# A decode attention block on one core: the tile steps as hardware loops of three tiles, and the rest as straight code ordered by a small tracker

## Chip, cores, metric

The kernel runs on one core of a Trainium2 chip. The metric is the device time of one execution in microseconds.

## The reference, cut to what matters

One token for each of two batch rows goes through cached attention with 32 heads, through a small mixer with an MLP, and the two results are mixed by a gate.

```python
B, Sq, D = 2, 1, 1024;  H, Sk, Dh = 32, 16384, 128
q = x @ wq
scores = einsum("bhqd,bhkd->bhqk", q, k_cache) * Dh ** -0.5
o = einsum("bhqk,bhkd->bhqd", softmax(scores), v_cache)
a = o @ wo
x1 = x + shifted(gelu(layernorm(x) @ w1)) @ w2        # one position: the shifted rows are all zero
b = x1 + gelu(layernorm(x1) @ w3) @ w4
out = g * a + (1 - g) * b                             # g = sigmoid(sum(x * gate_w))
```

The two caches are 537 MB in bf16, the weights some 36 MB. All of it is read once.

## The kernel before

The work is cut into 32 tiles of one batch row and two heads. A tile is one load of K and one of V, 8.39 MB each, and the loads go through three SBUF slots. VectorE transposes K in 16 pieces; PE multiplies each piece into the score bank S; then come the maximum, the exponentials and a transpose of the probabilities. While K of tile i+1 is scored, V of tile i is weighed.

```python
    def qk_stage(i):
        Kw = kn_tiles.pop(i)[:].bitcast(FP32)
        z = z_tiles[i % NZ]
        S = sps.tile([P, NC_], FP32, name="S")            # two score banks
        for m in range(NM):                               # NM = 16
            T = t_tile([P, 2, CJ, 32], FP32)              # two T buffers, in turn
            moved = nc.vector.transpose(out=T[:]..., in_=Kw[:, m * CW : (m + 1) * CW]...)
            for v in range(4):
                nc.tensor.matmul(S[:], lhsT=z[:, v, NM - 1 - m : NM - 1 - m + P], rhs=Tb[:, v // 2, :, v % 2],
                                 start=(m == 0 and v == 0), stop=(m == NM - 1 and v == 3))
    ...
    for i in range(-1, NT):                               # NT = 32, written out by Python: straight code
        if i + 1 < NT:
            xfers.append(("big", f"k{i + 1}", lambda i=i: load_k(i + 1)))
            steps.append((f"k{i + 1}", lambda i=i: (build_z(i + 1), qk_stage(i + 1))))
        if i >= 0:
            xfers.append(("big", f"v{i}", lambda i=i: load_v(i)))
            steps.append((f"v{i}", lambda i=i: pv_stage(i)))
        if i + 1 < NT:
            steps.append(("", lambda i=i: softmax_stage(i + 1)))
        if i in extra:                                    # w1 and w2 after tile 4, w3 after tile 8
            ...
```

The load of w2 is deliberately uneven: 216 of its 1024 rows go by a DMA whose slowest dimension is 3.

```python
    WAYS, QUAD, BASE, MORE = 3, 4, 6, 18
        nc.sync.dma_start(out=w2[:, 0:BASE, :], in_=B_w2[0 : P * BASE, :]...)
        nc.sync.dma_start(out=w2[W2_MORE, BASE : BASE + MORE, :],
            in_=B_w2[r0 : r0 + n_more, :].rearrange("(y x r) n -> x y (r n)", x=WAYS, y=QUAD))
        nc.sync.dma_start(out=w2[W2_REST, BASE, :], in_=B_w2[r0:D, :])
```

## Time and profile before

| | before |
|---|---|
| device time, median | 1334.2 us |
| span in the profile | 1332.4 us |
| DMA engines busy with data | 99.4% |
| PE / VectorE busy | 60% / 57% |
| last weight piece landed, first and last engine | 1321.4 and 1328.8 us |

The page's head, its 40 slices and its DMA queues. In the queue lines the columns are packets, MB, and the time of the packets as a share of the span of 16 engines.

```profile
span 1332.4 us, 11498 instructions
PE 797.2 (60%) x4982; PEld 354.1 (27%) x5045; DVE 760.4 (57%) x1005; ACT 27.2 (2%) x68; POOL 12.8 (1%) x40
...
DMA  9999999999999999999999999999999999999998
...
q1 hardware_dynamic: 11165, 572.53, 99.4%
q8 instruction: 39, 0.64, 0.2%
q14 instruction: 11, 0.09, 0.0%
```

Read the DMA line first: no slice of the span has the engines idle. PE (PEld is the loading of its weights) and VectorE (DVE) are each busy for under two thirds of it. The second thing to see is q8: instructions too are fetched by these DMA engines, 39 packets of 16 KB. They are taken here as those of PE's straight code of 10,162 instructions (5,045 weight loads, as many matmuls, 72 others), because the counts fit: between the packets at 84.9 and 1298.8 us PE starts 9,205 instructions, and 36 packets come, 255.7 instructions to each. So a packet is 256 instructions of 64 bytes; the sizes of loop bodies are estimates from that.

One tile on VectorE, from the timeline (start, duration, what, and in brackets the idle time before it and what ended that):

```profile
633.59 2.37 DVE L384 STREAM_TRANSPOSE T<-Kn 128x1024 f32<-128x1024 f32 x2 [6.85 <-DMA Kn<-in_A_k_cache_dram]
636.89 1.25 DVE L384 STREAM_TRANSPOSE T<-Kn 128x1024 f32<-128x1024 f32 x1 [0.93 <-PE S L398]
638.40 15.65 DVE L384 STREAM_TRANSPOSE T<-Kn 128x1024 f32<-128x1024 f32 x13 [0.27 <-PE S L398]
655.21 0.69 DVE L409 TENSOR_REDUCE m<-S 128x1 f32<-128x512 f32 x1 [1.15 <-PE S L398]
658.83 0.35 DVE L453 TENSOR_SCALAR Os<-O,xmask 128x128 f32<-128x128 f32 x1 [2.94 <-PE O L442]
...
665.01 0.17 DVE L477 RECIPROCAL rinv<-misc 128x2 f32<-128x2 f32 x1 [0.74 <-PE misc L251]
672.24 2.37 DVE L384 STREAM_TRANSPOSE T<-Kn 128x1024 f32<-128x1024 f32 x2 [7.06 <-DMA Kn<-in_A_k_cache_dram]
```

VectorE idles 7.06 us until the next K has landed. The period is 38.65 us, which is two loads of 19.3 us.

The view of waits (engine and line, what was waited for, us in total, times, longest):

```profile
DVE T L384 <- DMA Kn<-in_A_k_cache_dram: 203.8, 30, 12.5
```

A third reading comes from the times of the DMAs' semaphore updates in the trace. Each load of K or V, and each of the last weight pieces, posts 16 updates, read here as one for each engine that has finished its share. Sorted, for the last weight piece of the kernel before, in us of the span:

```
1321.42 1321.47 1321.75 1321.99 | 1326.91 1327.32 1327.46 1327.56 1328.08 1328.21 1328.35 1328.38 1328.40 1328.48 1328.65 1328.80
```

Four engines are done 5 to 7 us before the others. A load is complete only with its last engine (the first update for the K of the tile above comes at 628.05 us, the sixteenth at 633.57, and VectorE starts at 633.59), so the end of the kernel follows the most loaded engine and not the mean. How the engines came apart can be followed. After the first instruction packet, at 31.7 us, one engine finishes the next load 1.82 us behind the first and 1.25 behind the last but one; the weights before it came within 0.6. From there the spread is 2 us until the uneven w2 load, 5.5 us right after it (three engines late), and then the other nine catch up with those three over the remaining millisecond and mostly pass them, to 7.4 us.

### The profile page before, as it was taken

How to read it: one execution, taken by the hardware profiler on the slowest of the kernel's cores; microseconds unless marked ns; L12 is line 12 of the kernel's file. 1: busy time of each engine (PE TensorE's matmuls, PEld its weight loads, DVE VectorE, ACT ScalarE, POOL GpSimd, SP SyncE). 2: the span in 40 equal slices, each digit the busy share in tenths (PEclk: the TensorE clock that was granted, in tenths of full speed). 3: DMA queues.
4: the chain of work that ended last, by engine and by line, in shares of the span. 5: the costliest groups of instructions: out<-in, count | busy, mean ns of one | idle time of the engine just before them, and what ended most of it. 6: DMA issues, size and time to landing. Idle time of an engine off the chain costs nothing.

```text
span 1332.4 us, 11498 instructions
## 1 busy us (share of the span) xinstructions
PE 797.2 (60%) x4982; PEld 354.1 (27%) x5045; DVE 760.4 (57%) x1005; ACT 27.2 (2%) x68; POOL 12.8 (1%) x40
## 2 busy tenths in 40 slices
PE   2576655766556755556665555566655556655554
PEld 1223222322225322222222222222222222222222
DVE  1677665466653665555666555566655556665540
ACT  0000000000000000000000000000000000000000
POOL 0000000000000000000000000000000000000000
PEclk9788877787777777788887777888777788877776
DMA  9999999999999999999999999999999999999998
GB/s 410 439 437 435 422 437 432 426 435 433 437 428 441 431 422 439 439 437 425 431 436 433 439 429 437 424 439 433 433 431 438 438 424 435 437 437 430 431 427 340
DMA packets 11221, 573.27 MB, mean 430 GB/s; under 512 B 1252, under 2 KB 1260, under 8 KB 1687
## 3 DMA queue, kind: packets, MB, share of 16 engines
q1 hardware_dynamic: 11165, 572.53, 99.4%
q8 instruction: 39, 0.64, 0.2%
q14 instruction: 11, 0.09, 0.0%
q10 hardware_dynamic: 6, 0.01, 0.0%
HBM read 572.53 MB, written 0.00 MB: 430 GB/s over the span
## 4 chain that ended last, share of the span: by engine, by line
PE 33%; DVE 30%; DMA 21%; another core or an unknown queue 12%; issue 3%; ACT 1%; ACTq 0%; SPq 0%; DVEq 0%
DVE T L384 23%; PE S L398 21%; DMA Kn<-in_A_k_cache_dram 14%; PE O L442 7%; DMA wt<-in_B_w_dram 4%; DMA wo<-in_A_wo_dram 2%; PE misc L251 2%; DMA w<-in_B_w_dram 2%; DVE Os L457 2%; ACT Pr L426 1%; DVE PT L430 1%; PE misc L613 1%; DVE mx L419 1%; PE misc L594 1%
## 5 line engine op out<-in xcount | busy, mean ns | idle before, releaser
L398 PE MATMUL S<-T,z 128*128 128x512 bf16 x1985 | 580.6, 420 | 330.5 <-DVE T L384 308.8
L384 DVE STREAM_TRANSPOSE T<-Kn 128x1024 f32<-128x1024 f32 x512 | 612.0, 1229 | 254.9 <-DMA Kn<-in_A_k_cache_dram 203.8
L398 PEld LDWEIGHTS <-z 128*128 128x128 bf16 x2048 | 210.5, 104 | 687.1 <-issue 524.1
L442 PE MATMUL O<-Vn,PT 128*32 128x512 bf16 x2048 | 120.1, 388 | 7.1 <-DMA Vn<-in_A_v_cache_dram 7.1
L442 PEld LDWEIGHTS <-PT 128*32 128x32 bf16 x2048 | 73.8, 140 | 52.7 <-issue 16.5
L453 DVE TENSOR_SCALAR Os<-O,xmask 128x128 f32<-128x128 f32 x32 | 11.2, 350 | 103.8 <-PE O L442 103.8
L251 PE MATMUL misc<-rs,ones_f 128*128 128x2 f32 x64 | 17.9, 349 | 79.4 <-DVE rs L473 79.4
L426 ACT ACTIVATE Pr<-S,nb 128x512 bf16<-128x512 f32 x32 | 22.0, 687 | 1199.4 <-DVE nb L421 1161.7
L465 PE MATMUL misc<-asel,Os 128*128 128x2 f32 x64 | 12.2, 261 | 51.9 <-DVE Os L457 51.9
L409 DVE TENSOR_REDUCE m<-S 128x1 f32<-128x512 f32 x32 | 22.1, 692 | 35.8 <-PE S L398 35.8
L430 DVE STREAM_TRANSPOSE PT<-Pr 128x512 bf16<-128x512 bf16 x32 | 22.8, 711 | 29.0 <-ACT Pr L426 29.0
L251 PEld LDWEIGHTS misc<-rs,ones_f 128*128 128x128 f32 x64 | 16.0, 311 | 84.3 <-issue 81.5
L457 DVE SCALAR_TENSOR_TENSOR Os<-O,xmask,Os 128x128 f32<-128x128 f32 x96 | 33.6, 351 | 3.4
L465 PEld LDWEIGHTS misc<-asel,Os 128*128 128x128 f32 x64 | 9.5, 188 | 66.4 <-DVE Os L457 62.1
L251 PE MATMUL misc<-mdiag,ones_f 128*128 128x128 f32 x64 | 15.5, 325 | 17.1 <-DVE mdiag L412 17.1
L419 DVE TENSOR_REDUCE mx<-misc 64x1 f32<-64x64 f32 x64 | 14.2, 222 | 19.1 <-PE misc L251 18.7
L358 POOL TENSOR_TENSOR z<-qsel,own 128x32 bf16<-128x32 bf16 x32 | 10.7, 336 | 1200.3 <-PE S L398 1171.0
L613 PE MATMUL misc<-xn2T,wt 128*128 128x2 bf16 x224 | 14.4, 202 | 7.3 <-DMA wt<-in_B_w_dram 7.3
L477 DVE RECIPROCAL rinv<-misc 128x2 f32<-128x2 f32 x32 | 5.4, 170 | 23.1 <-PE misc L251 23.1
L714 DVE CAST T<-out_acc 128x256 bf16<-128x256 f32 x1 | 0.4, 423 | 28.0 <-PE out_acc L502 28.0
L613 PEld LDWEIGHTS <-wt 128*128 128x128 bf16 x224 | 14.3, 172 | 7.5 <-DMA wt<-in_B_w_dram 7.5
L480 DVE SCALAR_TENSOR_TENSOR OT<-misc,g_bc,rinv 128x2 bf16<-128x2 f32 x32 | 7.0, 219 | 15.4 <-PE misc L465 15.4
(91 smaller groups left out, 120.4 us busy)
## 6 DMA issues: line engine op xcount, KB each, us to landing
wt<-in_B_w_dram SPq DMA_DIRECT2D x1, 7168.0 KB
w<-in_B_w_dram SPq DMA_DIRECT2D x2, 3584.0 KB
wo<-in_A_wo_dram SPq DMA_DIRECT2D x3, 2048.0 KB, 41.9
wt<-in_B_w_dram SPq DMA_DIRECT2D x1, 2048.0 KB, 37.4
wt<-in_B_w_dram SPq DMA_DIRECT2D x1, 1536.0 KB, 41.0
wo<-in_A_wo_dram SPq DMA_DIRECT2D x1, 1024.0 KB, 46.1
Kn<-in_A_k_cache_dram SPq DMA_DIRECT2D x32, 51.6
Vn<-in_A_v_cache_dram SPq DMA_DIRECT2D x32, 37.2
```

The source lines that it names most:

```text
L251: nc.tensor.matmul(ps[:], lhsT=ones_f[:], rhs=src, start=True, stop=True)
L384: moved = nc.vector.transpose(out=T[:].rearrange("p w j s -> p j w s"), in_=Kw[:, m * CW : (m + 1) * CW].rearrange("p (j w e) -> p j w e", ...
L398: nc.tensor.matmul(S[:], lhsT=z[:, v, NM - 1 - m : NM - 1 - m + P], rhs=Tb[:, v // 2, :, v % 2], start=(m == 0 and v == 0), stop=(m == NM ...
L409: nc.vector.reduce_max(out=m[:], in_=S[:], axis=AX.X)
L419: nc.vector.reduce_max(out=mx[pa, :], in_=mall[pa, pa], axis=AX.X)
L426: nc.scalar.activation(out=Pr[:], in_=S[:], func=ACTF.Exp, bias=nb[:], scale=scale, accum_out=rs[:])
L430: nc.vector.transpose(out=PT[:], in_=Pr[:])
L442: nc.tensor.matmul(O[32 * g : 32 * g + 32, :], lhsT=PT[:, m : CJ * 32 : 16], rhs=V[:, j0 : j0 + 4, :], start=(m == 0), stop=(m == NM - 1),)
L457: nc.vector.scalar_tensor_tensor(out=Os[:], in0=Ox, scalar=xmask[:, x : x + 1], in1=Os[:], op0=ALU.mult, op1=ALU.add,)
L465: nc.tensor.matmul(oc[:], lhsT=Os[:], rhs=asel[:], start=True, stop=True)
L594: nc.tensor.matmul(ps[group(g), :], lhsT=actT[rows, r, :], rhs=w[rows, r, g * HW : (g + 1) * HW], start=False, stop=(n == len(slots) - 1), ...
L613: nc.tensor.matmul(ps[:, c, :], lhsT=w[:, r, :].rearrange("k (p c) -> k p c", c=C)[:, :, c], rhs=actT[:, r, :], start=(r == 0), stop=(r == ...
```

## The change

The intent, as far as the code shows it, is to shorten the program. 30 of the 32 tiles become hardware loops on PE and VectorE, three tiles to a body because there are three slots, with hand-made counting semaphores. Everything else stays straight code, but its waits come from a small dependency tracker and not from the framework. Four more things change on the way: w1, w2 and w3 are loaded first and their stages run before the first tile; w2 is loaded evenly; there is one score bank and not two; and the step writes its result at a register's address.

```diff
-    for i in range(-1, NT):
-        ... (steps written out, see above)
+    def pe_loop():
+        pe = nc.tensor
+        with pe.Fori(0, LOOP, NBIG):                      # LOOP = 30, NBIG = 3
+            got = Count(pe, sem["to_pe"])
+            for t in range(NBIG):
+                for m in range(NM):
+                    for v in range(4):
+                        ins = score(pe, m, v)
+                        if v == 0:
+                            got.next(ins)
+                        if v == 3:
+                            ins.then_inc(sem["to_dve"], 1)
+                take(pe, v_in[t], 16)
+                ... (weigh V, join heads, two sums)
+            got.take_off()                                # lowers the counters for the next round
+    def dve_loop():
+        dve = nc.vector
+        with dve.Fori(0, G * LOOP, G * NBIG) as place:
+            ...
+            for t in range(NBIG):
+                take(dve, k_in[t], 16)
+                for m in range(NM):
+                    ins = turn_k(dve, k_slot[t + 1], m)
+                    if m >= 2:
+                        got.next(ins)
+                    ins.then_inc(sem["to_pe"], 1)
+                got.next(top(dve)).then_inc(sem["own_dve"], 1)
+                mine.next().then_inc(sem["free"], 1)      # the K slot is free
+                ...
+                got.next(put_head(dve, bass.DynSlice(place + G * t, G))).then_inc(sem["free"], 1)
+                ...
-        nc.sync.dma_start(out=w2[W2_MORE, ...], ...)      # uneven
+    wq = load_pieces(wq_slot, 0, A_wq, [KC])
+    w1 = load_pieces(w12_slot, 0, B_w1, [KC])
+    w2 = load_pieces(w12_slot, KC * D, B_w2, [KC])        # even
+    w3 = load_pieces(next_slot(), 0, B_w3, [KC])
+    ...
+    st_mix(w1, w2)
+    st_up(w3)
+    note_scores(K)                                        # tile 0, straight code
```

## The prediction

> **What bounds it now.** The DMA stream. The page shows the 16 DMA engines busy 99.4% by the data queue at 430 GB/s; 572.5 MB are read whatever the program does. Successive 8.39 MB cache loads land 19.30 us apart (trace: semaphore updates of the DMAs), 434.7 GB/s, so the bytes alone need about 1317 us. A tile brings two loads, 38.6 us. Its compute chain (timeline, 599.2 to 626.7 us) takes only 27.5 us: transposes with score matmuls to 616.8, weighing and head sums to 622.5, softmax to 626.7. VectorE then waits about 7 us for the next K (waits view). The V load is issued some 18 us, the K load some 32 us, before the queue would run dry. PE (60% busy) and VectorE (57%) are off the critical path; what counts is whether the queue starves, and how much the most loaded DMA engine carries.
>
> That second part can be read: the last weight piece lands on the first engine at 1320.8 us, on the last at 1328.2. Four engines are 5 to 7 us ahead. The difference is instruction fetch (39 packets of 16 KB, 0.94 us each, some 1.25 us of delay to their engine) on nine engines, and the lopsided w2 load on three others.
>
> **What the change does.**
> 1. PE and VectorE loop over 30 of the 32 tiles. PE's body is about 815 instructions. [...]No run here shows a loop yet. [...]If bodies are refetched, fetches rise to 47-60: 1 to 4 us later on the loaded engines. If the body stays resident, they fall to about 10: some 4 us earlier.
> 2. w2 becomes an even load: about 1 us more on the nine engines, 4 us less on three.
> 3. w1, w2, w3 come first; their stages run before the first tile. From the durations before (mixer stage 16 us, w3 product 14.4 us): K1's load is issued near 48 us, V0's near 70 (needed at 88), K2's near 92 (needed at 107), V1's near 122 (needed at 126.5). Dense, with 5 us to spare at V1; a bubble of up to 4 us is possible.
> 4. One S bank instead of two, VectorE's waits on itself, register-addressed output, two barriers: 1 to 3 us a tile, inside the 11 us of slack. Freed-slot signals come 2 us later: inside 18 us.
> 5. The tail (last weight piece to the end, 4.2 us) stays.
>
> **Time.** No refetch: about 1330; refetch spread over the engines: 1335 to 1338; concentrated on few: up to 1345. I say 1333.5 us, 80% range 1327 to 1344. Faster by over 2%: 1%; within 2%: 94%; slower: 5%.
>
> **What would show it.** DMA busy stays at 98-99% and 427-432 GB/s; loads land every 19.30 us from the third tile on; VectorE still waits for K in each tile; 16 KB instruction packets number near 10 or near 50, and the engines' last landings spread less or more with them.
>
> **What would make it wrong.** Fetch stalls well over 11 us per tile would make PE the bound and cost tens of us; a starved queue at the start; or loop waits that serialise transposes and matmuls, so that a tile takes over 38.6 us.

## More of the kernel before

The times of one kernel agree within a few tenths of a microsecond. Where they do not (one run of the written-out loops, the uneven w2 in the changed kernel, the 14 reductions) the range is given.

## The result

1331.43 us (1331.32 to 1331.63, four runs) against 1334.24 us. The ratio is 0.9979, interval 0.9962 to 0.9996; here and below a ratio is the mean time of one kernel's fast runs over that of the other's of the same rounds, so not quite the ratio of the medians quoted. The gain is 2.8 us, 0.2%, well outside the run-to-run scatter of both kernels and far inside "same" at 2%.

The page after, the same lines:

```profile
span 1329.4 us, 11487 instructions
PE 805.7 (61%) x4957; PEld 318.0 (24%) x5011; DVE 761.2 (57%) x1007; ACT 27.2 (2%) x68; POOL 12.8 (1%) x40
...
DMA  9999999999999999999999999999999999999998
...
q1 hardware_dynamic: 11100, 572.53, 99.5%
q8 instruction: 11, 0.18, 0.0%
q14 instruction: 4, 0.03, 0.0%
```

The same work was executed (11,487 instructions against 11,498), and the DMA line is as full as before. What differs is q8: 11 instruction packets in place of 39. Their times in the trace say more: seven lie between 31.5 and 181.8 us, then none for over a millisecond, and four after 1263 us, when the tail begins. The seventh still belongs to the first pass through the loop, which ends near 199 us. From there on PE branches back nine times without fetching. The queue q14 fell too, from 11 packets to 4. They are of 8 KB and take 0.31 us each; their number would fit the instructions of the other engines (1,399 before, by the same 64 bytes 128 to a packet), but the trace names none.

One tile on VectorE, and the total of its waits for K:

```profile
630.56 2.37 DVE L507 STREAM_TRANSPOSE T<-slot 128x1024 f32<-128x1024 f32 x2 [7.05 <-DVEq L899]
633.79 1.25 DVE L507 STREAM_TRANSPOSE T<-slot 128x1024 f32<-128x1024 f32 x1 [0.86 <-PE S L516]
...
652.86 0.69 DVE L525 TENSOR_REDUCE m<-S 128x1 f32<-128x512 f32 x1 [1.17 <-PE S L516]
656.49 0.35 DVE L578 TENSOR_SCALAR mix<-O,xmask 128x128 f32<-128x128 f32 x1 [2.94 <-PE O L567]
...
662.46 0.17 DVE L563 RECIPROCAL rinv<-tot 128x2 f32<-128x2 f32 x1 [0.68 <-PE tot L533]
669.20 1.25 DVE L507 STREAM_TRANSPOSE T<-slot 128x1024 f32<-128x1024 f32 x1 [6.57 <-DVEq L899]
```
```profile
DVE T L507 <- DVEq L899: 190.9, 29, 7.4
```

"DVEq" needs care. In the loop the wait for K is an instruction of VectorE's sequencer (line 899 is `take`: wait for 16, then take them off), so the profile names that and no longer the DMA. It is still the wait for K: loads land 19.3 us apart from the first tile to the last. The chain of this tile is 32.1 us (630.56 to 662.63), half a microsecond longer than that of the tile shown before. That is not the change: from tile to tile the chain varies between 31.3 and 32.2 us in both kernels. Over 20 tiles from 437 us on, its mean is 31.85 us before and 31.76 after, and VectorE then waits 6.86 and 6.87 us for K. The change costs a tile nothing that can be seen.

The last weight piece, engine by engine:

```
1322.11 1322.12 1322.14 1322.37 1322.63 1322.72 1322.85 | 1323.47 1323.58 1323.59 1323.65 1323.66 1323.69 1323.74 | 1325.10 1325.21
```

The spread has gone from 7.4 to 3.1 us, and the last engine is done 3.6 us earlier. From there to the end of the span it takes 4.2 us where it took 3.6, so 0.6 us are given back, which leaves the 3.0 us between the two spans.

At the start, the loads are issued as follows (start, time until the last of the group was issued, what):

```profile
28.59 18.89 SPq L80 DMA_DIRECT2D slot<-in_A_k_cache_dram  x2
69.75 0.33 SPq L80 DMA_DIRECT2D slot<-in_A_v_cache_dram  x1
92.71 0.33 SPq L80 DMA_DIRECT2D slot<-in_A_k_cache_dram  x1
121.91 0.33 SPq L80 DMA_DIRECT2D slot<-in_A_v_cache_dram  x1
```

K0 and K1, V0, K2, V1. When V1 is issued at 121.9, K2 is still arriving, and its first engine finishes at 126.2: 4.3 us to spare, of which a part is needed for the load to get going (see the uneven w2 in the changed kernel).

### The profile page after: what moved, and what is told of

It reads as the page before. It is cut to its first block, busy times and chain, and to the rows that moved or that the text cites. A ratio compares the mean times of both kernels' runs of the same rounds, so it can differ in the third digit from the quotient of the medians.

```text
span 1329.4 us, 11487 instructions
## 1 busy us (share of the span) xinstructions
PE 805.7 (61%) x4957; PEld 318.0 (24%) x5011; DVE 761.2 (57%) x1007; ACT 27.2 (2%) x68; POOL 12.8 (1%) x40
## 5 line engine op out<-in xcount | busy, mean ns | idle before, releaser
L507 DVE STREAM_TRANSPOSE T<-slot 128x1024 f32<-128x1024 f32 x480 | 574.5, 1230 | 240.4 <-DVEq L899 190.9
L516 PEld LDWEIGHTS S<-T,z 128*128 128x128 bf16 x1920 | 165.7, 104 | 676.6 <-DVE T L507 516.5
L567 PE MATMUL O<-slot,PT 128*32 128x512 bf16 x1920 | 110.5, 383 | 0.0
L567 PEld LDWEIGHTS O<-slot,PT 128*32 128x32 bf16 x1920 | 69.0, 140 | 41.2 <-issue 13.3
L533 PE MATMUL tot<-rs,ones_f 128*128 128x2 f32 x60 | 17.6, 363 | 73.9 <-DVE rs L558 73.9
L80 DVE STREAM_TRANSPOSE T<-slot 128x1024 f32<-128x1024 f32 x32 | 38.2, 1227 | 11.0 <-DMA slot<-in_A_k_cache_dram 7.1
L550 ACT ACTIVATE mix<-S,nb 128x512 bf16<-128x512 f32 x30 | 20.6, 687 | 1119.5 <-DVE nb L540 1119.5
L555 DVE STREAM_TRANSPOSE PT<-mix 128x512 bf16<-128x512 bf16 x30 | 21.3, 711 | 25.3 <-ACT mix L550 25.3
L533 PEld LDWEIGHTS tot<-rs,ones_f 128*128 128x128 f32 x60 | 15.0, 312 | 79.7 <-DVE rs L558 79.7
L581 DVE SCALAR_TENSOR_TENSOR mix<-O,xmask,mix 128x128 f32<-128x128 f32 x90 | 31.6, 351 | 3.2
L533 PE MATMUL mall<-mix,ones_f 128*128 128x128 f32 x60 | 14.7, 326 | 13.4 <-DVE mix L528 13.4
L80 PEld LDWEIGHTS S<-T,z 128*128 128x128 bf16 x128 | 11.2, 105 | 41.6 <-DVE T L80 27.1
```

What stands on the lines that cost most here:

```text
L80: op = Op(engine, lambda: getattr(eng, method)(*args, **kwargs), reads, writes, waits, signal)
L507: return vector.transpose(out=t_tile([P, 2, CJ, 32], FP32, m % 2).rearrange("p w j s -> p j w s"), in_=K[:].bitcast(FP32)[:, m * CW : (m + ...
L516: return tensor.matmul(S, lhsT=z[:, v, NM - 1 - m : NM - 1 - m + P], rhs=Tb[:, v // 2, :, v % 2], start=(m == 0 and v == 0), stop=(m == NM ...
L533: return tensor.matmul(ps, lhsT=ones_f[:], rhs=src, start=True, stop=True)
L550: return scalar.activation(out=Pr, in_=S, func=ACTF.Exp, bias=stat["nb"][:], scale=scale, accum_out=stat["rs"][:])
L555: return vector.transpose(out=PT[:], in_=Pr)
```

## The experiments

Theory A: the time is set by the most loaded DMA engine; the loops took instruction fetch off these engines, and that is the gain. Rivals: B, the new order of the stages, the tracker or the single score bank made it; C, the even w2 made it. Each run is compared with the kernel before on the same chip in the same rounds (before: 1334.2 us). Where a difference is under 2 us I use medians and ranges, because the intervals of the ratios are wider than that.

| run | 16 KB packets | last landing, first engine / last engine | median us (range) |
|---|---|---|---|
| before | 39 | 1321.4 / 1328.8 | 1334.2 (1334.0 to 1334.6) |
| after | 11 | 1322.1 / 1325.2 | 1331.4 (1331.3 to 1331.6) |
| before, w2 even | 39 | 1321.8 / 1329.2 | 1334.6 (1334.4 to 1334.7) |
| after, loops written out | 39 | 1322.0 / 1329.4 | 1335.7 (1335.6 to 1337.4) |
| after, body of 6 tiles | 14 | 1322.3 / 1325.4 | 1331.4 (1331.3 to 1331.7) |
| after, body of 15 tiles | 41 | 1322.1 / 1331.5 | 1338.0 (1337.8 to 1338.2) |

### The loops written out

```diff
-        with pe.Fori(0, LOOP, NBIG):
+        for n in range(0, LOOP, NBIG):
-                take(pe, v_in[t], 16)
+                pe.wait_ge(v_in[t], 16 * (n // NBIG + 1))
```
(and likewise on VectorE, with a fixed slice where the register was.)

> The changed kernel with both loops written out 10 times as straight code (same order, waits, buffers; waits count up instead of being taken off). Theory A, instruction fetch made the gain: the 16 KB instruction packets rise from 11 to about 39, the last weight piece lands on the slowest DMA engine at 1328.5 to 1329.5 us instead of 1325.2, and the time is 1334.5 to 1336 us, slower than the kernel before, as w2 is even here. Rival B, the new order of the stages, the tracker or the single score bank made it: 1331 to 1332 us.

Measured: 1335.69 us, 39 packets, last landing 1329.38. The page's queue lines of this run:

```profile
q1 hardware_dynamic: 11100, 572.53, 99.3%
q8 instruction: 39, 0.64, 0.2%
```

Theory A's numbers came out, rival B's did not. The trace shows where the time goes: over 20 tiles from 437 us on, the chain is 31.70 us, as in the loop (31.76), but the tiles are 38.87 us apart and not 38.64, because the last engine's share of K comes later and later. Everything in the change but the loops, taken together, makes the kernel slower than before by 1.5 us; the loops alone take off 4.3 us.

### The kernel before with an even w2

```diff
-        nc.sync.dma_start(out=w2[:, 0:BASE, :], ...)      # and W2_MORE, W2_REST
+        nc.sync.dma_start(out=w2, in_=B_w2.rearrange("(p r) n -> p r n", p=P))
```

> The kernel before with w2 loaded evenly by all 16 engines. Theory A: the nine engines that fetch instructions carry some 25 to 33 KB more each, 0.9 to 1.2 us, so the last landing goes from 1328.2 to 1329.2 and the time to about 1335.2 us; it should agree with the straight-code version within 0.7 us. Rival C, the lopsided w2 load itself was what held the kernel before back: 1331 to 1332 us.

Measured: 1334.62 us, last landing 1329.20. Rival C is out: the uneven load was no burden but a help of some 0.4 us (1334.4 to 1334.7 us against 1334.1 to 1334.6 in the same rounds). The effect is under half of what I expected. The two landings, 1328.80 and 1329.20, agree with it.

The agreement with the written-out loops within 0.7 us was missed: they are 1.07 us apart. Their last landings are 0.2 us apart (1329.20 and 1329.38), so the stream of data is no worse for the new order, the tracker and the single bank. The rest is at the two ends: the first load is issued at 0.96 us in place of 0.73 in the changed kernel and its variants, and from the last landing to the end they take 4.2 us in place of 3.4. In the trace of the changed kernel the last store lands at 1327.8, and 1.6 us of barriers and semaphore clearing follow; in the kernel before it is 1.0 us. This is read from traces; no run takes it apart.

So the 2.8 us are made of +0.4 (even w2), +1.1 (start and end of the hand-ordered section, as read from traces) and -4.3 (loops). The loops take off PE's packets (39 to 11, of 16 KB) and those of q14 (10 to 4, of 8 KB); every run with loops changes PE's and VectorE's together, so the two shares are not separated, but PE's is by far the larger in bytes.

### A longer body

```diff
-        with pe.Fori(0, LOOP, NBIG):
+        with pe.Fori(0, LOOP, 15):                         # and 6
-            for t in range(NBIG):
+            for t in range(15):
```

> The changed kernel with loop bodies of 15 tiles run twice (PE body some 4070 instructions, 260 KB, in place of 815, 52 KB). [...]the body doesn't stay, about 39 packets of 16 KB, 1334 to 1336 us. If it keeps any size of body: about 23 packets, 1332 to 1333 us.

> The changed kernel with loop bodies of 6 tiles run 5 times (PE body some 1630 instructions, 104 KB). [...]the body stays, 14 or 15 packets of 16 KB, 1331.4 to 1332.2 us. If what it keeps is smaller than 104 KB: about 39 packets, 1334.5 to 1338 us.

Measured for 15 tiles: 1337.97 us and 41 packets, slower than every other version but the one with 14 reductions below. For 6 tiles: 1331.37 us and 14 packets. The q8 line of 15 tiles first, then that of 6:

```profile
q8 instruction: 41, 0.67, 0.2%
```
```profile
q8 instruction: 14, 0.23, 0.1%
```

A body of 1630 instructions (104 KB) stays with PE, a body of 4070 (260 KB) does not. The time of the 15-tile body was 2 us above what I expected, and above the straight code with about as many packets. The landings show where: two engines stand alone at the end, at 1330.5 and 1331.5, 9.4 us behind the first, where the others are done by 1329.4; in the straight code the last is at 1329.4. The first engine is as early as ever (1322.1), so the queue of loads never ran dry and a stall at the branch is not the cause: at the only branch back VectorE begins 0.7 us after its K has landed. So it is less the count of packets than where they fall, as far as the trace shows; no run places them at will. The 6-tile body says the same in the other direction: three packets more than the changed kernel, the same last landing within 0.2 us, the same time.

### The uneven w2 in the changed kernel

```diff
-    w2 = load_pieces(w12_slot, KC * D, B_w2, [KC])
+    WAYS, QUAD, BASE, MORE = 3, 4, 6, 18                   # the three loads of before
```

> The changed kernel with the lopsided w2 load of before (three engines take 147 KB each more). Theory A: there is little fetch left to balance, so the three engines become the last, near 1326.5 us, and the time is 1332 to 1333 us. Rival: a lopsided load helps whenever there are loops too: 1330 to 1330.5 us.

Measured: 1335.51 us, spread over 1333.67 to 1336.3; only the run with 14 reductions scattered as much. Both expectations were missed, and for a reason that I had named in the prediction and then overlooked in making this kernel. The uneven w2 has 25 row slots where the even one has 8, so its product takes 50 matmuls and 11.0 us in place of 16 and 3.6, and this now stands ahead of the first tile. The issue of the first loads, and the GB/s in the 40 slices:

```profile
29.30 26.76 SPq L80 DMA_DIRECT2D slot<-in_A_k_cache_dram  x2
78.08 0.33 SPq L80 DMA_DIRECT2D slot<-in_A_v_cache_dram  x1
100.98 0.33 SPq L80 DMA_DIRECT2D slot<-in_A_k_cache_dram  x1
130.15 0.33 SPq L80 DMA_DIRECT2D slot<-in_A_v_cache_dram  x1
```
```profile
GB/s 412 425 435 366 439 439 417 436 438 438 438 428 427 438 436 438 434 422 438 436 438 436 421 440 436 438 436 424 434 436 438 438 428 428 438 436 438 434 419 352
```

V1 is issued 8.2 us later than in the changed kernel, at 130.15, while the first engine had finished K2 at 125.7. The engines run dry, the fourth slice falls to 366 GB/s, and the load that should land 19.3 us after K2 takes its first engine 25.7 us. The run says nothing about the balance of w2, since the dry spell also levelled the engines (5.6 us of spread at K2, 1.7 at V1). But it measures the slack at the start. V1's data must have begun to flow near 132.1 (its first landing at 151.4 less 19.3), 1.9 us after the issue. So of the 4.3 us of the changed kernel some 2.4 were usable, by this estimate, and 8.2 us were too much.

### Less slack in the loop

```diff
+                for n in range(8):                         # and 14
+                    dve.reduce_max(out=junk[:, n : n + 1], in_=S, axis=AX.X)
```
after the last instruction of each tile in VectorE's loop.

> The changed kernel with 8 useless reductions of the score bank on VectorE after each tile's softmax in the loop, 0.69 us each plus gaps, 5.8 us a tile. Theory A (DMA is the bound and VectorE waits 7.05 us per tile for the next K): hidden, 1331.3 to 1332.5 us. If a later freed-slot signal mattered anywhere: 1335 us or more.

> The same with 14 reductions, 10.2 us a tile. With 7.05 us of slack, as the waits of VectorE in the trace read: a tile takes 41.8 us instead of 38.63, about 28 tiles lose 3.15 us each, 1405 to 1430 us. With 11 us of slack, as the prediction had it: still 1331.3 to 1332.5 us.

Measured: 1331.44 us with 8, 1372.25 us (1370.08 to 1372.97) with 14. With 8, the wait for K in the view of waits shrinks and the time does not move:

```profile
DVE T L508 <- DVEq L900: 51.6, 25, 2.6
```

With 14 it is gone. The timeline of VectorE:

```profile
611.48 8.44 DVE L957 TENSOR_REDUCE junk<-S 128x1 f32<-128x512 f32 x14
619.84 2.36 DVE L508 STREAM_TRANSPOSE T<-slot 128x1024 f32<-128x1024 f32 x2
...
651.15 8.44 DVE L957 TENSOR_REDUCE junk<-S 128x1 f32<-128x512 f32 x14
659.51 2.36 DVE L508 STREAM_TRANSPOSE T<-slot 128x1024 f32<-128x1024 f32 x2
```

My 1405 to 1430 us were missed because I had the cost of the reductions wrong: back to back they take 0.60 us each, so 14 add 8.44 us and not 10.2. Over 20 tiles in the middle of the loop VectorE now starts the next K 8.28 us after the tile's last step, where it was 6.87; the tiles are 40.04 us apart and not 38.64. So 30 tiles lose 1.4 us each, 42 us; measured are 41 in the median and 39 in the profiled run. The slack of a tile is 7 us, and the prediction's 11 us is refuted: with 11 us this run would have stood at 1331.4. Note the brackets as well: at the first transposes of a tile no idle time is left.

### Better balance

Three runs tried to use the engines that are still done early. The first cuts w2 so that three engines take 53 KB more and the thirteen others 12 KB less, in runs of 4 KB (`WAYS, QUAD, BASE, MORE = 3, 16, 7, 2`). The second does it in runs of 16 KB (`3, 4, 7, 8`) and moves the zeroing of `shT` ahead of the first product, for which PE waited 4.2 us in the changed kernel. The third spreads the extra load over seven engines (`7, 4, 6, 8`, 37 KB more on seven, 29 KB less on nine). The changed kernel ran beside the last two.

> The changed kernel with a mildly lopsided w2: three engines take 53 KB (2 us) more, the thirteen others 12 KB (0.45 us) less; cut so that the w2 product has 20 matmuls in place of 16 and the start doesn't starve. Theory A (the slowest engine's load sets the end; 3.1 us of spread in the changed kernel): the last landing falls from 1325.2 to about 1324.8, 1330.9 to 1331.1 us, a little better than both kernels. If the end doesn't follow the slowest engine: 1331.4 us.

> The changed kernel as it is, beside the next two on one chip: 1331.3 to 1331.6 us, last landing at 1325.2 us, 11 packets of 16 KB.

> The changed kernel with a mildly lopsided w2 in runs of 16 KB instead of 4 KB (three engines 53 KB, 2 us, more, thirteen 12 KB less), and the zeroing of shT moved ahead of the first product, so that the w2 product doesn't wait for the gelu and the start keeps its 4 us of slack with 32 matmuls. If the short runs of 4 KB made the miss of the run before: the last landing falls to 1324.8 to 1325.2, 1331.0 to 1331.4 us. If each extra DMA costs all engines some 0.5 us (two more here): 1332 to 1332.5 us.

> The same with seven engines taking 37 KB (1.4 us) more and nine 29 KB (1.06 us) less. If the seven lightly loaded engines of the changed kernel are the ones that a DMA split seven ways uses: last landing near 1324.2 to 1324.7, 1330.4 to 1331 us. If they are others: 1332 to 1333.5 us.

Measured: 1332.97 us for the first. Its first engine at the last landing is at 1323.3 in place of 1322.1, and its last at 1326.6: all engines lost time, although thirteen had less to carry. The changed kernel again: 1331.46 us (1331.36 to 1331.59). The second: 1331.33 us (1331.18 to 1331.48), its last landing at 1325.07 beside 1325.03. The third: 1333.04 us, last landing 1326.70 with a spread of 5.6 us.

So the 4 KB runs were a good part of the first one's miss, as the 16 KB version stands 1.6 us better. The two differ in the zeroing of `shT` as well, but the traces show the loss at once, behind the same number of loads: the first K lands on its first engine at 50.5 us with 4 KB runs, at 49.1 with 16 KB and at 49.0 in the changed kernel. The 16 KB version too only reaches the changed kernel: 0.13 us faster in the median, with overlapping ranges and the same last landing. It is the fastest version measured and not a gain worth its code. The third came out as expected for the case that a split by seven uses other engines than the seven that are lightly loaded. Which ones these are stays open, as the semaphore updates don't name the engine.

## Why the prediction was right

The forecast of 1333.5 us, with 1327 to 1344, held 1331.4 us, and "within 2%" was right. The mechanism was right too, but the number was a mean over branches of which I could not tell which would happen. That the range held says little: it was wide enough for either branch, the 15-tile body's 1338.0 us included.

1. **The bound.** Right. Loads land every 19.3 us throughout, before and after, and VectorE can lose 4.8 us in every tile of the loop without any effect on the time (the run with 8 reductions of 0.60 us).
2. **Loops and instruction fetch.** Both branches were costed: "If the body stays resident, they fall to about 10: some 4 us earlier." The count was 11 and the loops took off 4.3 us (1335.69 to 1331.43). I held the other branch for at least as likely. The runs decide against it for PE: bodies of 52 KB and 104 KB are not fetched again (11 and 14 packets in the whole run), a body of 260 KB is (41). Where between these two sizes the limit lies was not shown. The branch to refetching was not wrong in itself: the 15-tile body shows it, at 1338.0 us.
3. **Even w2.** The sign was right, the size was not: "about 1 us more on the nine engines" measured 0.4 us. "4 us less on three" came out, as far as sorted landings can show it: with the even w2 seven engines are done by 1322.4 us, where before four were done by 1322.0 and the fifth only at 1326.9.
4. **The start.** Right, step by step, for the issue times. K1 near 48, V0 near 70, K2 near 92, V1 near 122 were forecast from durations before; the trace has 47.5, 69.8, 92.7, 121.9. No bubble came, and a bubble did come when another 8.2 us were put there.
5. **One bank, own waits, register address.** Inside the slack, as said, and the cost does not show at all (a chain of 31.76 us against 31.85), where I had 1 to 3 us a tile, an estimate for which I had no trace. But the slack itself was misread: "inside the 11 us of slack". I had taken the chain to start at 599.2 us, at the edge of my window of the timeline, with three of the sixteen transposes already done. The chain is 31.8 us and the slack 7, as the waits of VectorE in the same text ("about 7 us") already said. Two numbers that should add up to the period of 38.6 did not, and I let them stand.
6. **The tail.** Wrong: "The tail (last weight piece to the end, 4.2 us) stays." It was 3.6 us, since I had read the last piece but one as the last; and it grew to 4.2 us, because the hand-ordered section ends with more barriers and more semaphores to clear (1.6 us after the last store's landing, against 1.0, as read from the traces). Together with 0.2 us at the start this gives back a part of the gain.

The predicted 1330 us for the case that happened is 1.4 us too low. Of this the tail is 0.6. The rest, by the trace and tested by no run, is on the last engine: after the instruction packets of the straight tail at 1291 and 1309 us, two engines that were already among the later ones fall back further. At the last cache load the slowest engine was 1.7 us behind the first, at the last weight piece 3.1 us.

## What to carry to other kernels

When the DMA engines are the bound, program text is data too: here a fetch of 256 instructions took 0.94 us of one of the 16 engines, set it back by 1.25 us (the first one of the kernel before), and the load completed with the slowest engine (1328.8 us, where the first was done at 1321.4), so look at the semaphore updates one by one and not only at the busy share. A hardware loop whose body the engine keeps takes that text off the DMA engines (11 packets for 39, and 4.3 us); here the body that it did not keep cost more than straight code (1338.0 against 1335.7 us). And a stage that is moved to the front of a stream of loads must be costed against the slack there, which was smaller here (some 2.4 us usable) than that of a tile (7 us).
